# Fused attention and two MLPs: behind attention all five engines take their instructions in written order, with weight words moved and a third word tile

## The chip, the cores and the metric

The kernel runs on one core of a Trainium2 chip. The metric is the device time of one execution in microseconds (us), as a median over runs. The core has five engines with a queue each: TensorE (PE, matmuls), VectorE (DVE), ScalarE (ACT), GpSimd (POOL) and SyncE (SP, which here issues almost all DMAs).

## The reference

Block-causal attention over 4 batches x 8 heads x 576 positions x 64, whose output is a matrix of 2304 tokens x 512; then two MLPs one after the other, each 512 -> 2048 -> 512. The weights are float64 on the host.

```
x = attention(q, k, v)                                  # 2304 x 512
h = x @ w_in;  g = max(h, 0) + alpha * min(h, 0);  y = g @ w_out      # first MLP
h = y @ w_in2; g = where(h > 0, h, exp(min(h, 0)) - 1); out = g @ w_out2   # second MLP
```

## The kernel before

**Tokens and chunks.** The tokens are cut into five units u of 512, 512, 512, 512 and 256 tokens, the 2048 hidden features into 16 chunks f of 128. The program has two parts. In the first, attention runs together with chunks 0 to 3 of the first MLP for units 0, 1 and 2 (generator `l1_beside`). The change concerns the second part, "behind attention": a list of 148 steps, one for each (kind, unit, chunk). In order: A3 (steps 0 to 7), A4 (8 to 15), B2 (16 to 27), B0 (28 to 39), B1 (40 to 51), D4 (52 to 59), D3 (60 to 67), then the second MLP, C2 (68 to 83), C0, C1, C3, C4. A letter with a digit is a kind and its unit; unit 4 has 256 columns.

**A step.** At step i PE makes h(i), 12 matmuls into one of three "h" banks of PSUM (L551 for the first MLP, L605 for the second). ACT and DVE make the gate of it: in the first MLP `neg` (ACT, L528), `g` (DVE, L531), its rounded copy (ACT, L535) and the remainder (POOL, L89); in the second `e` by exp (ACT, L609), two DVE operations (L610, L611), a copy (ACT, L614) and the remainder (DVE, L89). The two results go into one tile of a ring: "gs" has four, "gsl" three, and steps use them by turns. Then PE takes h(i)'s tile of three steps ago (`lag = 3`) and makes y(i-3), up to four groups of matmuls that add into "acc" banks (L655, L630). PE thus always runs h(i), y(i-3), h(i+1), y(i-2) and so on.

**Joins.** A kind's and unit's last y closes its sums, three steps after its last h. I call that step a join: step 10 (A3 to A4), 18 (A4 to B2), 30, 42, 54, 62 and 70 (D3 to C2). There the four sums leave the acc banks: `to_z` copies them at steps 10 and 18 (ACT for m = 0 and 2, tile `z`; DVE for m = 1 and 3, tile `zl`; L93 and L95), and stores them by DMA (L558); later joins add an earlier `z` (DVE, L662), round and store (L663, L665). There are five acc banks in a ring, of which a unit takes four, so that the next unit's second sum needs a bank that the join must have emptied.

**Weight words.** `load_w(layer, f, r)` brings one "word": 512 KB of float64, which arrives in a `wraw` tile (three of them, L123) and is turned into a rounded weight and its remainder: ACT twice (L133, L134), DVE three times (L138, L139, L143), POOL once (L148), ACT (L158), DVE (L89, out `w`). `later(n, ...)` puts each of these stages into a coming tick; a step has two ticks, so the stages stand one half step apart in the source, and the first stands `arrival[0]` ticks after the load. Word number k thus needs `wraw` from the load to L148 and a `wword` tile from L133 to the last L89. `w_at` says at which step which word is loaded.

**Order.** In the first part `manual_schedule` names all five engines: each takes instructions as the source emits them. In the second part only PE is named; for ACT, DVE, POOL and SP a planner, with its own estimates of times, has put instructions into an order at build time. On the chip an engine's queue is what was built.

Of the kernel before, what the change touches and what calls it, by code (L numbers as in the profile page):

```python
# [9 lines left out]
F32 = mybir.dt.float32  # L10
# [4 lines left out]
ALU = mybir.AluOpType  # L15
# [4 lines left out]
P = 128  # L20
B, H, S, D = 4, 8, 576, 64
NT, DM, DFF = 2304, 512, 2048
# [14 lines left out]
def f32(ap):  # L37
    return ap.bitcast(F32)
# [3 lines left out]
def attention_moe_kernel(ctx: ExitStack, tc: tile.TileContext, qT, kT, v_a, v_b, w1, w2, alpha, out):  # L42
    nc = tc.nc
    pe, act, dve, pool_e = nc.tensor, nc.scalar, nc.vector, nc.gpsimd
# [4 lines left out]
    wraw_p = ctx.enter_context(pool("wraw", 2))  # L49
# [18 lines left out]
    def ring(name, *banks):  # L68
        rings[name] = list(banks)
# [18 lines left out]
    def low_part(eng, out, x, high):  # L88
        return {"v": dve, "p": pool_e}[eng].tensor_tensor(out=out, in0=x, in1=f32(high), op=ALU.subtract)  # L89

    def copy(eng, out, x, scale=None):
        if eng == "a":
            return act.copy(out, x) if scale is None else act.mul(out, x, scale)  # L93
        if eng == "v":
            return dve.tensor_copy(out, x) if scale is None else dve.tensor_scalar(out, x, scale, None, ALU.mult)  # L95
        return pool_e.tensor_scalar(out, x, 1.0 if scale is None else scale, 1.0, ALU.mult, ALU.mult)  # L96
# [6 lines left out]
    def later(ticks, emit):  # L103
        due.setdefault(tick[0] + ticks, []).append(emit)
# [13 lines left out]
    def load_w(layer, f, r):  # L118
        if r == 0:
            wt[layer, f] = w_pools[min(f // 4, 2)].tile([P, 2, 2 * DM], F32R, tag="w", name="w")  # L120
        t = wt[layer, f]
        raw = wraw_p.tile([P, 2 * DM], U32, tag="wraw", name="wraw", bufs=3)
        nc.sync.dma_start(out=raw, in_=(w1, w2)[layer][f, :, r * DM:(r + 1) * DM].bitcast(U32))  # L123
        pairs = raw.rearrange("p (n t) -> p n t", t=2)
        low, high = pairs[:, :, 0], pairs[:, :, 1]
        units = low.bitcast(I32)
        hi, lo = (t[:, k, r * DM:(r + 1) * DM] for k in range(2))
        word = []

        def first():  # L130
            w = wraw_p.tile([P, DM], F32, tag="wword", name="wword")
            word.append(w)
            act.activation(out=w, in_=high.bitcast(F32), func=AF.Abs)  # L133
            act.activation(out=units, in_=low, func=AF.Copy, scale=2.0 ** -29)  # L134

        def bits():
            w, wi = word[0], word[0].bitcast(U32)
            dve.tensor_scalar(w, w, F64_MIN, F64_MAX, ALU.max, ALU.min)  # L138
            dve.tensor_scalar(wi, wi, 3, 0x3FFFFFF8, ALU.logical_shift_left, ALU.bitwise_and)  # L139

        def sign():
            wi = word[0].bitcast(U32)
            dve.scalar_tensor_tensor(  # L143
                out=wi, in0=high, scalar=0xC0000000, in1=wi, op0=ALU.bitwise_and, op1=ALU.bitwise_or)

        def rounded():
            w = word[0].bitcast(I32)
            pool_e.tensor_tensor(out=w, in0=w, in1=units, op=ALU.add)  # L148

        def last():  # L150
            low_part("v", lo, word[0], hi)
            ready.add((layer, f, r))
        lead = arrival[0]
        later(lead, first)
        later(lead + 1, bits)
        later(lead + 1, sign)
        later(lead + 2, rounded)
        later(lead + 3, lambda: act.copy(hi, word[0]))  # L158
        later(lead + 4, last)

    arrival = [2]
# [21 lines left out]
    ap2 = att.enter_context(pool("att2", 2))  # L183
# [18 lines left out]
        return d // 2, slice(4 * (d % 2), 4 * (d % 2) + 4)  # L202

    def raw_tiles():
        return [ap2.tile([P, S], F32, tag=f"{x}raw", name=f"{x}raw", bufs=4) for x in "qk"]

    def load_early(d):
        b, hs = duo(d)
# [15 lines left out]
    def load_late(n):  # L224
        b, p = PAIRS[n]
        st[n]["raw"] = q, k = raw_tiles()
        hs = slice(2 * p, 2 * p + 2)
        nc.sync.dma_start(out=k, in_=kT[b, hs].rearrange("e p s -> (e p) s"))
        nc.sync.dma_start(out=q[:, 256:], in_=qT[b, hs].rearrange("e p s -> (e p) s")[:, 256:])

    def load_late_v(n):
        b, p = PAIRS[n]
# [5 lines left out]
    def high_parts(n):  # L238
        s = st[n]
        q, k = s["raw"]  # L240
        for which, x, scale in (("q", q[:, 256:], 0.125), ("k", k, None)):
            s[which] = [ap2.tile([P, x.shape[1]], F32R, tag=f"{which}{t}", name=f"{which}{t}") for t in "hl"]
            copy("p", s[which][0], x, scale)
        low_part("p", s["k"][1], k, s["k"][0])

    def low_parts(n):
        s = st[n]
        hi, lo = s["q"]
        dve.scalar_tensor_tensor(out=lo, in0=s["raw"][0][:, 256:], scalar=0.125, in1=f32(hi), op0=ALU.mult, op1=ALU.subtract)

    def diagonal(n):
        for low in range(2):
# [189 lines left out]
    for n in range(NP):  # L442
        k = AT[n, EARLY]
# [3 lines left out]
        for i in (2, 3, 4):  # L447
            k = AT[n, i]
# [12 lines left out]
    for n in range(NP):  # L461
        k = NP + 3 * n
# [83 lines left out]
    def l1_h(u, f):  # L546
        n, x = UNITS[u], x1[u]
        h = bank[take("h")][:, :n]
        for kc in range(KC):
            for t, (wp_, xp_) in enumerate(PASSES):  # L550
                pe.matmul(h, w_in(0, f, wp_, kc), x[:, xp_, kc, :n],  # L551
                          start=kc == 0 and t == 0, stop=kc == KC - 1 and t == 2)
        return h
# [46 lines left out]
    def l2_h(u, f):  # L600
        n, x = UNITS[u], x1[u]
        h = bank[take("h")][:, :n]
        for kc in range(KC):
            for t, (wp_, xp_) in enumerate(PASSES):
                pe.matmul(h, w_in(1, f, wp_, kc), x[:, xp_, kc, :],  # L605
                          start=kc == 0 and t == 0, stop=kc == KC - 1 and t == 2)
        e = gp.tile([P, 512], F32, tag="g", name="e", bufs=3)[:, :n]
        gs = gs_tile()[:, :, :n]
        act.activation(out=e, in_=h, func=AF.Exp)  # L609
        dve.tensor_scalar(e, e, 1.0, -1.0, ALU.min, ALU.add)  # L610
        dve.scalar_tensor_tensor(out=e, in0=h, scalar=0.0, in1=e, op0=ALU.max, op1=ALU.add)  # L611

        def parts():
            act.copy(gs[:, 0, :], e)  # L614
            low_part("v", gs[:, 1, :], e, gs[:, 0, :])
        later(1, parts)
        return gs
# [50 lines left out]
    ET = mybir.EngineType  # L668
    with tc.manual_schedule(engines={ET.PE, ET.Activation, ET.DVE, ET.Pool, ET.SP}):
# [29 lines left out]
        k = LEAD  # L699
        for u, (a, b, c, d) in enumerate(stretches):  # L700
            assert a >= X_DONE[u]
            parts = l1_beside(u)
            for first, end, n in ((a, b, 2 * FA), (c, d, 2 * KC)):
                slots(k, first)
                k = first
                for j in range(n):
# [3 lines left out]
                    k = to  # L710
# [1 line left out]
        assert not held and not halves  # L712


    with tc.manual_schedule(engines={ET.PE}):


        att.close()
        ps = ctx.enter_context(pool("ps_all", 1, space=PSUM))
        bank[:] = [ps.tile([P, 512], F32, name=f"bank{i}") for i in range(8)]  # L720
        w_pools.append(ctx.enter_context(pool("w2", NF - 8)))
        late_pools.append(ctx.enter_context(pool("late", 1)))
        ring("h", 5, 6, 7)
        ring("acc", *range(5))
        units = [("A", 3), ("A", 4)] + [("B", u) for u in (2, 0, 1)] + [
            ("D", u) for u in (4, 3)] + [("C", u) for u in (2, 0, 1, 3, 4)]
        fs = CHUNKS
        steps = [(k, u, f) for k, u in units for f in fs[k]]
        first_of = {}
        for i, (k, u, f) in enumerate(steps):  # L730
            first_of.setdefault((k, u), i)
        lag = 3
        words = sorted((3 * r + f, f, r) for f in range(8) for r in range(2))
        w_at = dict(zip((1, 3, 4, 6, 7, 8, 10, 12, 14, 16, 18, 19, 21, 22, 24, 25), ((0, 8 + f, r) for _, f, r in words)))
        freed = first_of["B", 1] + 8
        for i in range(16):
            f, r = divmod(i, 2)
            w_at[first_of["B", 0] + 2 * i if i < 8 else freed + 2 * i - 16] = 1, f, r
            w_at[first_of["C", 2] - 4 + i] = 1, 8 + f, r
        gs = {}  # L740
        for i in range(len(steps) + lag):
            if i in w_at:
                arrival[0] = 4 if i < first_of["C", 2] - 4 else 2
                load_w(*w_at[i])
            if i < len(steps):
                k, u, f = steps[i]
                if f == fs[k][1]:
                    n = units.index((k, u)) + 1
                    if n < len(units) and units[n] != ("D", u):
                        (load_x2 if units[n][0] == "C" else load_x1)(units[n][1])  # L750
                gs[i] = l2_h(u, f) if k == "C" else l1_gate(f, l1_h(u, f), UNITS[u])
            end_tick()
            if i >= lag:
                k, u, f = steps[i - lag]
                if k == "C":
                    l2_y(u, f, gs.pop(i - lag))
                else:
                    l1_y(k, u, f, gs.pop(i - lag))
            end_tick()
# [32 lines left out]
```

## Time and profile before

| | |
|---|---|
| median of 3 runs | 1006.86 us (1006.8 to 1007.06) |
| the profiled execution's own time | 1007.81 us |
| its span, first to last instruction | 1006.0 us |
| PE busy | 961.3 us (96% of the span), granted clock 0.989 |
| DVE, ACT, POOL busy | 541.1, 441.9, 343.9 us |
| stretch 258 to 612 us (A, B, D): PE, DVE, ACT, POOL busy | 343.67, 196.31, 159.59, 156.82 of 354.00 us |
| stretch 612 to 1001 us (C): the same | 386.52, 155.90, 102.75, 12.00 of 389.00 us |

Read it as follows. PE is busy nearly always, and a matmul's end is modelled, so what counts is the distance from one start to the next and the idle times that a row gives in brackets. The time of an engine other than PE counts only where PE stands still for it.

### The profile page before, as it was taken

What the parts mean: (1) busy time and instruction counts of PE and PEld (TensorE: products, weight loads), DVE (VectorE), ACT (ScalarE), POOL (GpSimd) and SP (SyncE); (2) the same over time, 40 slices, a digit from 0 to 9 for tenths busy, and PEclk for the clock granted to TensorE, in tenths of its full rate; (3) what the DMA queues carried; (4) which work ended last, traced back from release to release, by engine and by line L of the source; (5) the groups of instructions that cost most, each with busy time, mean ns of one, the idle gap of its engine ahead of it and who ended that gap; (6) DMA issues with size and microseconds to landing.
All of it is one profiled execution on the core that took longest, in us unless ns stands there. A gap on an engine that the chain in (4) does not pass through costs nothing.

```text
span 1006.0 us, 13778 instructions
## 1 busy us (share of the span) xinstructions
PE 961.3 (96%) x5008; PEld 774.1 (77%) x5008; DVE 541.1 (54%) x1012; ACT 441.9 (44%) x985; POOL 343.9 (34%) x401
## 2 busy tenths in 40 slices
PE   5789999999997999999999999999999999999997
PEld 3456777666787788888889887888888888888896
DVE  5878676776498871311862489634333333333343
ACT  6876576776465653222553365422222222222222
POOL 4788576694255553322553363200000000000000
PEclk9999999999998999999999999999999999999999
DMA  6553533625546552401535555002002100200010
GB/s 216 178 183 140 154 102 114 224 72 157 183 140 237 199 183 84 141 0 42 186 119 177 163 201 174 29 1 111 15 1 84 42 1 1 84 1 0 1 43 21
DMA packets 55525, 105.76 MB, mean 105 GB/s; under 512 B 11041, under 2 KB 29473, under 8 KB 54305
## 3 DMA queue, kind: packets, MB, share of 16 engines
q1 hardware_dynamic: 55168, 104.62, 31.4%
q8 instruction: 39, 0.64, 0.3%
q10 hardware_dynamic: 288, 0.26, 0.1%
q14 instruction: 30, 0.24, 0.1%
HBM read 76.55 MB, written 28.31 MB: 104 GB/s over the span
## 4 chain that ended last, share of the span: by engine, by line
PE 73%; DVE 11%; ACT 6%; DMA 4%; POOL 3%; issue 2%; SPq 0%; POOLq 0%; ACTq 0%; DVEq 0%
PE bank L630 20%; PE bank L605 19%; PE bank L655 11%; PE bank L551 11%; PE bank L423 3%; PE bank L582 3%; DMA wraw<-w 2%; DVE w L89 2%; PE bank L570 2%; DVE wword L143 2%; PE pair L276 2%; DVE wword L139 2%; PE bank L363 2%; DVE wword L138 1%; ACT wword L133 1%
## 5 line engine op out<-in xcount | busy, mean ns | idle before, releaser
L605 PE MATMUL bank<-x,w 128*128 128x512 f32 (+1 forms) x960 | 210.4, 368 | 0.0
L605 PEld LDWEIGHTS bank<-x,w 128*128 128x128 f32 x960 | 169.7, 189 | 31.4
L551 PE MATMUL bank<-x,w 128*128 128x512 f32 (+1 forms) x816 | 177.2, 367 | 1.3 <-DVE xtail L89 1.3
L551 PEld LDWEIGHTS bank<-x,w 128*128 128x128 f32 x816 | 143.0, 191 | 26.2 <-ACT xtail L429 1.4
L610 DVE TENSOR_SCALAR e<-e 128x512 f32<-128x512 f32 (+1 forms) x80 | 33.1, 413 | 172.1 <-ACT e L609 172.1
L609 ACT ACTIVATE e<-bank 128x512 f32<-128x512 f32 (+1 forms) x80 | 44.4, 555 | 184.8 <-PE bank L605 184.8
L148 POOL TENSOR_TENSOR wword<-wword,wraw 128x512 int32<-128x512 int32 x64 | 93.7, 1465 | 77.3 <-issue 23.5
L531 DVE SCALAR_TENSOR_TENSOR g<-neg,beta,bank 128x512 f32<-128x512 f32 (+1 forms) x80 | 55.1, 689 | 117.8 <-ACT neg L528 117.7
L630 PE MATMUL bank<-w,gsl 128*128 128x512 f32 x432 | 106.4, 393 | 2.2 <-DVE z L662 2.2
L630 PE MATMUL bank<-w,gs 128*128 128x512 f32 x432 | 104.6, 389 | 0.0
L655 PE MATMUL bank<-gsl,w 128*128 128x512 f32 (+1 forms) x408 | 91.0, 371 | 9.1 <-ACT z L93 6.5
L96 POOL TENSOR_SCALAR p<-p,stat 128x128 f32<-128x128 f32 (+4 forms) x144 | 81.3, 580 | 48.5 <-DVE stat L334 32.7
L630 PEld LDWEIGHTS bank<-w,gsl 128*128 128x128 f32 x432 | 81.2, 190 | 19.5 <-DVE z L662 2.6
L630 PEld LDWEIGHTS bank<-w,gs 128*128 128x128 f32 x432 | 80.6, 188 | 16.4
L89 POOL TENSOR_TENSOR gs<-g,gs 128x512 fp32r<-128x512 f32 (+1 forms) x46 | 59.0, 1283 | 90.0 <-ACT gs L535 89.9
L655 PEld LDWEIGHTS bank<-gsl,w 128*128 128x128 f32 x408 | 71.7, 192 | 23.0 <-ACT z L93 7.1
L325 ACT ACTIVATE p<-pair,stat 128x128 f32<-128x128 f32 (+4 forms) x144 | 78.3, 557 | 24.0 <-DVE stat L298 21.7
L655 PE MATMUL bank<-gs,w 128*128 128x512 f32 (+1 forms) x408 | 87.8, 364 | 0.0
L655 PEld LDWEIGHTS bank<-gs,w 128*128 128x128 f32 x408 | 70.6, 189 | 12.2
L528 ACT ACTIVATE neg<-bank 128x512 f32<-128x512 f32 (+1 forms) x80 | 44.1, 552 | 79.5 <-PE bank L551 78.3
L89 DVE TENSOR_TENSOR w<-wword,w 128x512 fp32r<-128x512 f32 x64 | 57.1, 896 | 16.5 <-ACT w L158 15.9
L298 DVE TENSOR_REDUCE stat<-pair 128x2 f32<-128x256 f32 (+3 forms) x80 | 63.1, 806 | 4.2 <-PE pair L281 2.2
(80 smaller groups left out, 1256.7 us busy)
## 6 DMA issues: line engine op xcount, KB each, us to landing
wraw<-w SPq DMA_DIRECT2D x64, 512.0 KB, 4.0
xd<-x SPq DMA_DIRECT2D x4, 2048.0 KB, 8.5
x<-xd SPq DMA_DIRECT2D x16, 512.0 KB, 7.6
x<-yd SPq DMA_DIRECT2D x4, 2048.0 KB, 7.9
vraw<-v_a SPq DMA_DIRECT2D x24, 256.0 KB, 3.3
kraw<-kT SPq DMA_DIRECT2D x16, 288.0 KB, 3.8
yd<-gs SPq DMA_DIRECT2D x8, 512.0 KB, 3.7
yd<-gsl SPq DMA_DIRECT2D x8, 512.0 KB, 5.4
```

Of the source, the lines that this page charges most:

```text
L89: return {"v": dve, "p": pool_e}[eng].tensor_tensor(out=out, in0=x, in1=f32(high), op=ALU.subtract)
L96: return pool_e.tensor_scalar(out, x, 1.0 if scale is None else scale, 1.0, ALU.mult, ALU.mult)
L148: pool_e.tensor_tensor(out=w, in0=w, in1=units, op=ALU.add)
L298: peak = lambda out, x, axis=AX.X: dve.tensor_reduce(out=out, in_=x, axis=axis, op=ALU.max, negate=True)
L325: act.activation(out=out, in_=x, func=AF.Exp, bias=stat[:, k:k + 1], accum_out=stat[:, SUMS + 2 * k:SUMS + 2 * k + 1])
L528: act.activation(out=neg, in_=h, func=AF.Relu, scale=-1.0)
L531: dve.scalar_tensor_tensor(out=g, in0=neg, scalar=beta[:, f:f + 1], in1=h, op0=ALU.mult, op1=ALU.add)
L551: pe.matmul(h, w_in(0, f, wp_, kc), x[:, xp_, kc, :n], start=kc == 0 and t == 0, stop=kc == KC - 1 and t == 2)
L605: pe.matmul(h, w_in(1, f, wp_, kc), x[:, xp_, kc, :], start=kc == 0 and t == 0, stop=kc == KC - 1 and t == 2)
L609: act.activation(out=e, in_=h, func=AF.Exp)
L630: pe.matmul(acc, gs[:, gp_, tg * P:(tg + 1) * P], w_out(1, f, wp_, 0, DM), start=f == 0 and t == 0, stop=f == NF - 1 and t == 2)
L655: pe.matmul(acc, w_out(0, f, wp_, m * P, P), gs[:, gp_, :n], start=first and t == 0, stop=last and t == 2)
```

## The change

The second part's `manual_schedule` now names all five engines. `w_at` has new steps, in the diff. The first six words of the part are loaded in steps 0 to 5 with 6 ticks from load to first stage (before: 4). `wword` gets a third tile. To make room the late pairs' `q` is kept in a tile of 512 columns and not 576, at columns 0 to 319. No instruction of computation is added or removed; PE's order is the same row for row.

```diff
-            w = wraw_p.tile([P, DM], F32, tag="wword", name="wword")
+            w = wraw_p.tile([P, DM], F32, tag="wword", name="wword", bufs=3)
...
-        return [ap2.tile([P, S], F32, tag=f"{x}raw", name=f"{x}raw", bufs=4) for x in "qk"]
+        return [ap2.tile([P, n], F32, tag=f"{x}raw", name=f"{x}raw", bufs=4) for x, n in (("q", 512), ("k", S))]
...
-        nc.sync.dma_start(out=q[:, 256:], in_=qT[b, hs].rearrange("e p s -> (e p) s")[:, 256:])
+        nc.sync.dma_start(out=q[:, :320], in_=qT[b, hs].rearrange("e p s -> (e p) s")[:, 256:])
...
-    with tc.manual_schedule(engines={ET.PE}):
+    with tc.manual_schedule(engines={ET.PE, ET.Activation, ET.DVE, ET.Pool, ET.SP}):
...
-        w_at = dict(zip((1, 3, 4, 6, 7, 8, 10, 12, 14, 16, 18, 19, 21, 22, 24, 25), ((0, 8 + f, r) for _, f, r in words)))
-        freed = first_of["B", 1] + 8
-        for i in range(16):
-            f, r = divmod(i, 2)
-            w_at[first_of["B", 0] + 2 * i if i < 8 else freed + 2 * i - 16] = 1, f, r
-            w_at[first_of["C", 2] - 4 + i] = 1, 8 + f, r
+        w_at = dict(zip((0, 1, 2, 3, 4, 5, 9, 11, 13, 17, 18, 20, 21, 22, 24, 25), ((0, 8 + f, r) for _, f, r in words)))
+        w_at.update(zip((29, 31, 33, 35, 37, 41, 43, 45, 47, 48, 49, 53, 55, 57, 61, 62),
+                        ((1, f, r) for f in range(8) for r in range(2))))
+        w_at.update(zip((*range(64, 69), *range(71, 82)), ((1, 8 + f, r) for _, f, r in words)))
...
-                arrival[0] = 4 if i < first_of["C", 2] - 4 else 2
+                arrival[0] = 6 if i < 6 else 4 if i < first_of["C", 2] - 4 else 2
```

ACT's queue at the join of step 10 (A3 to A4), before; `neg<-bank_2977` is h(10)'s gate, `bank_2971` and `bank_2973` hold A3's sums 0 and 2:

```order
L158 CAST w<-wword 128x512
L133 ACTIVATE wword<-wraw 128x512
L134 ACTIVATE wraw<-wraw 128x512
L535 CAST gs<-g 128x256
L133 ACTIVATE wword<-wraw 128x512
L134 ACTIVATE wraw<-wraw 128x512 x2
L528 ACTIVATE neg<-bank_2977 128x256
L93 COPY z<-bank_2971 128x512
L158 CAST w<-wword 128x512
L535 CAST gsl<-g 128x256
L93 COPY z<-bank_2973 128x512
```

The same place in the changed kernel:

```order
L158 CAST w<-wword 128x512
L535 CAST gs<-g 128x256
L528 ACTIVATE neg<-bank_2977 128x256
L535 CAST gsl<-g 128x256
L93 COPY z<-bank_2971 128x512
L93 COPY z<-bank_2973 128x512
L133 ACTIVATE wword<-wraw 128x512
L134 ACTIVATE wraw<-wraw 128x512
```

The two copies now stand together, ahead of any stage of a word; five instructions on words (L133 twice, L134 three times) that stood ahead of the first copy behind the last L158 are gone from there.

DVE's queue at the join of step 70 (D3 to C2), before; `bank_2975`, `bank_2971`, `bank_2972`, `bank_2973` hold D3's four sums, `bank_2977` is h(70):

```order
L89 TENSOR_TENSOR gs<-e,gs 128x512
L138 TENSOR_SCALAR wword<-wword 128x512
L662 TENSOR_TENSOR z<-bank_2975,z 128x512
L610 TENSOR_SCALAR e<-e 128x512
L662 TENSOR_TENSOR zl<-bank_2971,zl 128x512
L139 TENSOR_SCALAR wword<-wword 128x512
L662 TENSOR_TENSOR z<-bank_2972,z 128x512
L611 SCALAR_TENSOR_TENSOR e<-bank_2977,e 128x512
L89 TENSOR_TENSOR w<-wword,w 128x512
L662 TENSOR_TENSOR zl<-bank_2973,zl 128x512
L89 TENSOR_TENSOR gs<-z,gs 128x512
```

The same place in the changed kernel:

```order
L610 TENSOR_SCALAR e<-e 128x512
L611 SCALAR_TENSOR_TENSOR e<-bank_2977,e 128x512
L89 TENSOR_TENSOR gsl<-e,gsl 128x512
L662 TENSOR_TENSOR z<-bank_2975,z 128x512
L89 TENSOR_TENSOR gs<-z,gs 128x512
L662 TENSOR_TENSOR zl<-bank_2971,zl 128x512
L662 TENSOR_TENSOR z<-bank_2972,z 128x512
L89 TENSOR_TENSOR gs<-z,gs 128x512
L662 TENSOR_TENSOR zl<-bank_2973,zl 128x512
L89 TENSOR_TENSOR w<-wword,w 128x512
```

The whole gate of h(70), remainder included, and the remainders of the sums now stand ahead of later sums; the words' stages L138 and L139 no longer stand between.

## Rows read from the trace of the kernel before

**Rows 1.** Waits of PE, 258 us to the end: total, times, longest.

```profile
PE bank L655 <- ACT z L93: 6.5, 2, 4.9
PE bank L630 <- DVE z L662: 2.2, 1, 2.2
```

**Rows 2.** PE timeline, undisturbed: start, us, line, operation, count.

```profile
324.08 1.60 PE L655 MATMUL bank<-gsl,w 128*128 128x256 f32 x12
325.52 1.60 PE L551 MATMUL bank<-x,w 128*128 128x256 f32 x12
...
402.96 2.88 PE L551 MATMUL bank<-x,w 128*128 128x512 f32 x12
405.68 2.88 PE L655 MATMUL bank<-gsl,w 128*128 128x512 f32 x12
```

**Rows 3.** PE timeline, the join A3 to A4.

```profile
310.22 0.52 PE L655 MATMUL bank<-gsl,w 128*128 128x256 f32 x3
...
321.21 1.60 PE L655 MATMUL bank<-gs,w 128*128 128x256 f32 x12
```

**Rows 4.** PE timeline, the join A4 to B2.

```profile
346.57 0.84 PE L655 MATMUL bank<-gsl,w 128*128 128x512 f32 x3
...
356.72 2.88 PE L655 MATMUL bank<-gs,w 128*128 128x512 f32 x12
```

**Rows 5.** PE timeline, the join D3 to C2.

```profile
613.82 0.84 PE L630 MATMUL bank<-w,gsl 128*128 128x512 f32 x3
...
623.60 2.88 PE L630 MATMUL bank<-w,gs 128*128 128x512 f32 x12
```

**Rows 6.** PE timeline, the end of attention and steps 0 to 4.

```profile
247.36 0.52 PE L363 MATMUL bank<-ident,p 128*128 128x128 f32 x3 [0.79 <-ACT pt L93]
...
259.61 11.16 PE L551 MATMUL bank<-x,w 128*128 128x512 f32 x48 [1.26 <-DVE xtail L89]
270.61 0.40 PE L655 MATMUL bank<-gsl,w 128*128 128x512 f32 x1
...
274.49 2.88 PE L551 MATMUL bank<-x,w 128*128 128x512 f32 x12
```

**Rows 7.** ACT groups on words, 255 to 360 us: count | busy, mean ns | idle before, releasers.

```profile
L133 ACT ACTIVATE wword<-wraw 128x512 f32<-128x512 f32 x22 | 14.8, 670 | 9.5 <-DVE w L89 7.7 <-DMA wraw<-w 1.8
L134 ACT ACTIVATE wraw<-wraw 128x512 int32<-128x512 uint32 x21 | 14.3, 679 | 14.5 <-DMA wraw<-w 13.7 <-DVE pt L95 0.8
...
L158 ACT CAST w<-wword 128x512 fp32r<-128x512 f32 x21 | 12.9, 619 | 9.9 <-POOL wword L148 9.9
```

**Rows 8.** ACT timeline at the join A3 to A4.

```profile
310.51 0.62 ACT L158 CAST w<-wword 128x512 fp32r<-128x512 f32 x1 [2.83 <-POOL wword L148]
...
315.02 0.59 ACT L93 COPY z<-bank 128x512 f32<-128x512 f32 x1
```

**Rows 9.** DVE timeline at the join D3 to C2.

```profile
612.08 0.43 DVE L138 TENSOR_SCALAR wword<-wword 128x512 f32<-128x512 f32 x1 [0.40 <-ACT wword L133]
...
614.70 1.51 DVE L138 TENSOR_SCALAR wword<-wword 128x512 f32<-128x512 f32 x1
616.13 0.68 DVE L662 TENSOR_TENSOR z<-bank,z 128x512 f32<-128x512 f32 x1
```

**Rows 10.** POOL timeline at the same join.

```profile
614.41 1.52 POOL L148 TENSOR_TENSOR wword<-wword,wraw 128x512 int32<-128x512 int32 x1 [3.73 <-ACT wword L133]
```

**Rows 11.** ACT timeline around the end of attention.

```profile
240.54 0.69 ACT L134 ACTIVATE wraw<-wraw 128x512 int32<-128x512 uint32 x1 [1.93 <-DMA wraw<-w]
...
264.78 0.66 ACT L134 ACTIVATE wraw<-wraw 128x512 int32<-128x512 uint32 x1 [5.90 <-DMA wraw<-w]
```

**Rows 12.** Page, DMA issues: count, KB each, median us to landing.

```profile
wraw<-w SPq DMA_DIRECT2D x64, 512.0 KB, 4.0
```

**Rows 13.** Page, costliest groups: gate and remainder of the first MLP.

```profile
L531 DVE SCALAR_TENSOR_TENSOR g<-neg,beta,bank 128x512 f32<-128x512 f32 (+1 forms) x80 | 55.1, 689 | 117.8 <-ACT neg L528 117.7
...
L89 POOL TENSOR_TENSOR gs<-g,gs 128x512 fp32r<-128x512 f32 (+1 forms) x46 | 59.0, 1283 | 90.0 <-ACT gs L535 89.9
```

More of the change, by code (lines that the diff above doesn't have):

```diff
@@ L240, in high_parts @@
         q, k = s["raw"]
-        for which, x, scale in (("q", q[:, 256:], 0.125), ("k", k, None)):
+        for which, x, scale in (("q", q[:, :320], 0.125), ("k", k, None)):
             s[which] = [ap2.tile([P, x.shape[1]], F32R, tag=f"{which}{t}", name=f"{which}{t}") for t in "hl"]
@@ L248, in low_parts @@
         hi, lo = s["q"]
-        dve.scalar_tensor_tensor(out=lo, in0=s["raw"][0][:, 256:], scalar=0.125, in1=f32(hi), op0=ALU.mult, op1=ALU.subtract)
+        dve.scalar_tensor_tensor(out=lo, in0=s["raw"][0][:, :320], scalar=0.125, in1=f32(hi), op0=ALU.mult, op1=ALU.subtract)
     def diagonal(n):
```

## The prediction

> **What bounds the kernel now.** I read the waits of PE behind attention first. They are few: 6.5 us for ACT's copies of `z`, 2.2 us for DVE's adds [rows 1]. PE's order is the same before and after, so the time behind attention is PE's undisturbed pace plus what it loses at these places. The pace comes from starts in quiet stretches: twelve matmuls of 512 columns take 405.68 - 402.96 = 2.72 us, twelve of 256 columns 325.52 - 324.08 = 1.44 us [rows 2]. Next I read the PE timeline at each place where it waits, and took the way from the disturbed start to the next undisturbed one, less that pace; this counts the idle time and also the matmuls that run longer after it:
>
> - Join of A3 and A4: from y(8) at 310.22 to y(9) at 321.21 are 10.99 us [rows 3]; y(8) and h(12), 256 columns each, should take 2.88. Lost 8.11.
> - Join of A4 and B2: 346.57 to 356.72 are 10.15 us [rows 4]; y(16) and h(20) should take 5.44. Lost 4.71.
> - Join of D3 and C2: 613.82 to 623.60 are 9.78 us [rows 5], against 5.44. Lost 4.34.
> - First y of the part: 270.61 to 274.49 are 3.88 us [rows 6], against 2.72. Lost 1.16.
> - End of attention: 0.79 us for a copy on ACT [rows 6].
>
> Together 19.11 us. There is one more, the 1.26 us before step 0's first matmul, which waits for attention's last output [rows 6].
>
> Then I looked at why. An engine's instructions stand in one queue, and what waits at its head holds the rest. From 255 to 360 us ACT stood idle ahead of words' stages for 9.5 + 14.5 + 9.9 = 33.9 us, for DVE, for loads and for POOL [rows 7]. At the first join ACT sat 2.83 us for a word at POOL, until 310.51, and copied A3's first sum only at 315.02 [rows 8]. That sum was complete before 310.22, as PE was already at A4's first y then [rows 3]. So `z` is late because the planner put words ahead of it. At D3 to C2 it is DVE: L138 stands ahead of the first add and takes 1.51 us, since POOL's L148 runs from 614.41 to 615.93 meanwhile; alone the same instruction takes 0.43 [rows 9, 10]. Near 264.78 ACT waited 5.90 us for a load with the gate of h(0) behind it, and at 240.54 it waited 1.93 us so with attention's work behind it [rows 11].
>
> **The change, part by part.** *Joins of steps 10 and 18.* Let T be the end of h(10). In the new order ACT has the gate's `neg`, the copy and then both `z`, with no word between. An ACT operation of a full tile takes about 0.6 (L158: 619 ns [rows 7]), a `g` 0.69 [rows 13]. The first `z` is done by T + 0.6 + 0.7 + 0.6 + 0.6 = T + 2.5, even with full widths. PE wants its bank for the second sum of y(8): y(7) 2.72, h(11) 1.44, one sum of four 0.36, so T + 4.5. The other copies on ACT and DVE end near T + 3.2, for T + 4.9 and later. At step 18 the want is 1.44 + 2.72 + 0.68 = T + 4.8. Both losses go: -8.11 and -4.71. What hides the copies is one h; without it 2 us would show.
>
> *Join of step 70.* With T the end of h(70), DVE does `e` by T + 1.7 (ACT 0.6, DVE 0.4 and 0.7), waits for ACT's copy (2.3), makes the remainder (2.9), add 0 (3.6), waits for that copy (4.2) and makes its remainder (4.9), add 1 (5.6), add 2 (6.3). PE wants the banks at 5.44 + 0.68 = T + 6.1, then 6.8 and 7.5. It fits by 2.5, 1.2 and 1.2 us. But each collision with POOL adds 1.51 - 0.43 = 1.1 us [rows 9], and words come at one per step until step 68, so DVE may arrive late. From below 0 remains, from above all 4.34. I take 0.7, since one collision fits and a second does not quite: -3.6.
>
> [...]
>
> *Joins of steps 30, 42, 54, 62.* No wait of PE stands there now, and the same walk (no `e`; the remainder of g is POOL's) ends add 2 at T + 4.7 for a want of 7.5, at step 54 (256 columns behind it) of 2.72 + 1.44 + 1.08 = 5.2. There a collision would cost 0.6; I take 0.
>
> *A wait that the change adds.* A join takes two tiles of the gsl ring for its sums. The fourth sum's copy goes into the tile that y(i-2) reads, and PE runs that one step later. In written order ACT stands at it for some 5 us, with the next word and neg(i+1) behind; two steps on, the copy of g(i+2) waits in the same way for y(i), until T + 3 x 5.44 + 2.72 = T + 19.0. Who waits for these? y(i+2) wants its tile at T + 5 x 5.44 = T + 27.2, and the copy and POOL's 1.3 [rows 13] are over at T + 21. h(i+6) wants the bank of h(i+3) at T + 29.9, and its gate, with a word's 1.35 us on ACT ahead, is through by T + 23. PE does not see it: 0, with 6 us to spare.
>
> *SP.* Stores of `z` at a join now hold the loads behind them. The word of step 11 is issued near T + 3.5 and lands 4.0 us later [rows 12], or about T + 8 behind the stores; its L133 stands behind the gate of h(12), at T + 8.4 to 9. Words loaded in steps 0 to 5 have three steps, 16 us, from load to first stage. Each word is through about two steps before its first matmul. 0; a late one costs 5 us only where it eats these two steps.
>
> *Start.* Steps 0 to 2 now have no word's stage on ACT before them, so neg(0) follows h(0) at once: -1.16. Attention's last copies lose the two hoisted L134: -0.79. The third `wword` tile takes away L133's wait for DVE, 7.7 us of ACT there [rows 7], which lies beside PE; the narrower `q` moves the same bytes. Both 0 in themselves.
>
> Sum: -8.11 - 4.71 - 3.6 - 1.16 - 0.79 = -18.4. The profiled execution took 1007.81 us, its span 1006.0. It would take 989.4. The runs' median lies 0.95 us below that execution, so **988.4 us**.
>
> **The rivals.** *One join keeps its wait.* DVE comes to step 70 a few us behind, since with a word per step it has about 4 us of work plus collisions in 5.44. For it: the stretch's L138 of 1.51. Against it: no bits are placed in step 70. 988.4 + 3.6 = 992.0.
>
> *Loads hold ACT.* L133 and L134 waited 15.5 us for loads in that stretch [rows 7]; in written order a late one holds the gates behind it, and in A4's short steps the slack is three steps of 2.88, about 8.6 us. One wait such as the 5.90 [rows 11] fits, two in a row do not: some 6 us back, 994 to 995.
>
> *Slower: the gsl ring.* If a later gate, not only the copy, were held until the third step after a join, PE would stand at each of the five joins behind step 18. The slack of 6 us decides: a wait longer than 5 + 6 = 11 us reaches PE. A hold of a whole three-step round, 16 us, would cost 5 us each at five joins, 25 us: about 1013. Against it: the copy is freed by y(i), which itself waits for nothing behind it.
>
> [...]
>
> *It does nothing.* The waits could come from loads or banks whatever the order: 1007. Against it: the sum that PE waited for was complete some 5 us before its copy.
>
> **How the numbers follow.** All joins clear, 0.70, with a range of its own of 986.5 to 990.5 (step 70's 0 to 2 us, and about 1 us either way for attention's end). One join kept 0.13. Loads 0.09. Gsl ring 0.05. Nothing 0.03. A measurement of this kernel tells about 0.2%, 2 us, from no change. Faster 0.92, same 0.03, slower 0.05. The range, 986 to 994.5, takes in the first two cases and half of the third.
>
> **What would show it.** Right: after the profile, PE's waits behind attention hold only the 1.26 us, at most 2 us at step 70, and the starts between steps 8 and 20 are 1.44 and 2.72 us apart; ACT's `z` at step 10 ends within 3 us of h(10). ACT's idle time ahead of the join's fourth copy and of the copy two steps later, some 5 us each, shows the ring, with no PE wait after it. Wrong: PE waits for `neg` or `g` at h, or for `w`, or for a POOL remainder at a y, or new waits in attention's last 15 us.

## The result and the profile after

The changed kernel takes **989.41 us** (median of 6 runs, 988.59 to 990.09); the kernel before, beside it, 1006.44 us (6 runs, 1004.85 to 1007.06). The ratio is 0.9834, 95% interval 0.9821 to 0.9846. The profiled execution took 989.64 us, its span is 987.8 us (before 1006.0), PE is busy for 955.5 us of it (97%) at a granted clock of 0.995 (before 0.989), and the median landing time of a word is 4.6 us (before 4.0 [rows 12]).

Waits of PE from 255 us to the end, which answer to [rows 1] (total, times, longest):

```profile
PE bank L551 <- DVE xtail L89: 1.3, 1, 1.3
PE bank L551 <- DVE g L531: 0.6, 1, 0.6
```

The copies of `z` and the adds, 6.5 and 2.2 us before, are gone from the list. The first row is the one at step 0, which was there before; the second is new. The PE timeline (start, us, line, operation, count, idle time) at step 0, at the joins of steps 10, 18 and 70, and at the new wait, step 60 (h of D3's first chunk):

```profile
258.78 11.16 PE L551 MATMUL bank<-x,w 128*128 128x512 f32 x48 [1.27 <-DVE xtail L89]
269.78 2.88 PE L655 MATMUL bank<-gsl,w 128*128 128x512 f32 x12
272.50 2.88 PE L551 MATMUL bank<-x,w 128*128 128x512 f32 x12
...
308.24 1.60 PE L655 MATMUL bank<-gsl,w 128*128 128x256 f32 x12
...
311.12 1.60 PE L655 MATMUL bank<-gs,w 128*128 128x256 f32 x12
...
336.48 2.88 PE L655 MATMUL bank<-gsl,w 128*128 128x512 f32 x12
...
341.92 2.88 PE L655 MATMUL bank<-gs,w 128*128 128x512 f32 x12
...
538.77 1.60 PE L655 MATMUL bank<-gsl,w 128*128 128x256 f32 x12
541.01 3.01 PE L551 MATMUL bank<-x,w 128*128 128x512 f32 x12 [0.64 <-DVE g L531]
543.86 1.60 PE L655 MATMUL bank<-gs,w 128*128 128x256 f32 x12
...
599.94 2.88 PE L630 MATMUL bank<-w,gsl 128*128 128x512 f32 x12
...
605.38 2.88 PE L630 MATMUL bank<-w,gs 128*128 128x512 f32 x12
```

From y(8) to y(9) are 311.12 - 308.24 = 2.88 us, where [rows 3] show 10.99; at step 18, 5.44 where [rows 4] show 10.15; at step 70, 605.38 - 599.94 = 5.44 where [rows 5] show 9.78; behind the first y, 2.72 where [rows 6] show 3.88. All four run at the undisturbed pace. Step 0 starts 259.61 - 258.78 = 0.83 us earlier. Step 60 loses 2.24 - 1.44 = 0.80, and 0.10 more in the matmuls behind it. So 0.83 + 8.11 + 4.71 + 1.16 + 4.34 - 0.90 = 18.25 us, against 1006.0 - 987.8 = 18.2 us of span.

ACT at the join of step 10; h(10) ends at 304.21:

```profile
304.31 0.39 ACT L528 ACTIVATE neg<-bank 128x256 f32<-128x256 f32 x1 [2.05 <-PE bank L551]
305.25 0.41 ACT L535 CAST gsl<-g 128x256 fp32r<-128x256 f32 x1 [0.55 <-DVE g L531]
305.56 0.58 ACT L93 COPY z<-bank 128x512 f32<-128x512 f32 x1
306.32 0.59 ACT L93 COPY z<-bank 128x512 f32<-128x512 f32 x1 [0.18 <-PE bank L655]
306.81 0.68 ACT L133 ACTIVATE wword<-wraw 128x512 f32<-128x512 f32 x1
```

The two `z` are done 1.9 and 2.7 us after h(10)'s end, within the 3 us forecast, and no word stands ahead. Before, the same first copy ran at 315.02 [rows 8]. DVE at the join of step 70, with h(70) ending at 594.66:

```profile
597.84 0.68 DVE L662 TENSOR_TENSOR z<-bank,z 128x512 f32<-128x512 f32 x1
...
599.82 0.68 DVE L662 TENSOR_TENSOR zl<-bank,zl 128x512 f32<-128x512 f32 x1
600.42 0.68 DVE L662 TENSOR_TENSOR z<-bank,z 128x512 f32<-128x512 f32 x1
601.79 1.28 DVE L89 TENSOR_TENSOR gs<-z,gs 128x512 fp32r<-128x512 f32 x1 [0.69 <-ACT gs L663]
```

Adds 0, 1 and 2 (L662) end 3.9, 5.8 and 6.4 us after h(70), for a want of 6.1, 6.8 and 7.5. One remainder takes 1.28 (0.69 for the one at 599.21), but behind the adds that count.

The new wait starts on SP. The word loaded in step 55 stands there behind the stores of join 54; ACT then waits for it with the gate of h(57) behind, and h(60) writes into the bank that this gate reads (SP rows: start, us in the queue, line; then ACT):

```profile
532.19 0.51 SPq L665 DMA_DIRECT2D yd<-gsl  x1
532.75 0.60 SPq L123 DMA_DIRECT2D wraw<-w  x1
...
538.92 0.68 ACT L133 ACTIVATE wword<-wraw 128x512 f32<-128x512 f32 x1 [1.85 <-DMA wraw<-w]
...
540.08 0.36 ACT L528 ACTIVATE neg<-bank 128x256 f32<-128x256 f32 x1
```

### The profile page after: what moved, and what is told of

Read it like the earlier page. It is cut to its first block, busy times and chain, and to the rows that moved or that the text cites. A ratio compares the mean times of both kernels' runs of the same rounds, so it can differ in the third digit from the quotient of the medians.

```text
span 987.8 us, 13766 instructions
## 1 busy us (share of the span) xinstructions
PE 955.5 (97%) x5008; PEld 770.9 (78%) x5008; DVE 545.7 (55%) x1012; ACT 437.4 (44%) x985; POOL 337.9 (34%) x401
## 4 chain that ended last, share of the span: by engine, by line
PE 85%; DVE 4%; POOL 3%; ACT 3%; issue 2%; DMA 1%; SPq 1%; POOLq 0%; ACTq 0%; DVEq 0%
PE bank L605 20%; PE bank L630 20%; PE bank L551 16%; PE bank L655 16%; PE bank L423 3%; PE bank L582 3%; PE pair L276 2%; PE bank L363 2%; PE bank L570 2%; ACT p L325 1%; POOL p L96 1%; DVE stat L298 1%; PE pair L281 1%; POOL gs L89 1%; PE bank L369 1%
## 5 line engine op out<-in xcount | busy, mean ns | idle before, releaser
L148 POOL TENSOR_TENSOR wword<-wword,wraw 128x512 int32<-128x512 int32 x64 | 93.3, 1458 | 79.1 <-DVE wword L143 61.6
L655 PE MATMUL bank<-gsl,w 128*128 128x512 f32 (+1 forms) x408 | 87.8, 364 | 0.0
L89 POOL TENSOR_TENSOR gs<-g,gs 128x512 fp32r<-128x512 f32 (+1 forms) x46 | 56.8, 1235 | 87.3 <-ACT gs L535 87.3
L89 DVE TENSOR_TENSOR w<-wword,w 128x512 fp32r<-128x512 f32 x64 | 67.1, 1048 | 16.6 <-ACT w L158 16.6
L143 DVE SCALAR_TENSOR_TENSOR wword<-wraw,wword 128x512 uint32<-128x512 uint32 x64 | 72.4, 1131 | 2.2
```

Of the source, the lines that this page charges most:

```text
L143: dve.scalar_tensor_tensor(out=wi, in0=high, scalar=0xC0000000, in1=wi, op0=ALU.bitwise_and, op1=ALU.bitwise_or)
L655: pe.matmul(acc, w_out(0, f, wp_, m * P, P), gs[:, gp_, :n], start=first and t == 0, stop=last and t == 2)
```

## The experiments

Three edits can be taken apart: who orders the queues, the third `wword` tile, and the steps of the words (with `arrival[0]`). The narrower `q` is in every cell of the table but the two with two tiles and old steps. No run has it alone; the program built with it alone has the same instructions in the same order on all five engines as before. This is what the eight combinations took, as ratios to the kernel before run beside each:

| word tiles | word steps | planner's order | written order |
|---|---|---|---|
| 2 | old | 1 (before) | 1.0111 (1.0086 to 1.0135) |
| 2 | new | 0.9987 (0.9976 to 0.9998) | 0.9976 (0.9964 to 0.9988) |
| 3 | old | 1.0125 (1.0094 to 1.0156) | 0.9905 (0.9886 to 0.9925) |
| 3 | new | 1.0093 (1.0061 to 1.0124) | 0.9834 (0.9821 to 0.9846), the change |

### The changed kernel with the planner's order

```diff
-    with tc.manual_schedule(engines={ET.PE, ET.Activation, ET.DVE, ET.Pool, ET.SP}):
+    with tc.manual_schedule(engines={ET.PE}):
```

> The changed kernel with the new word steps, the third word tile and the narrower q, but with ACT, DVE, POOL and SP behind attention ordered by the planner again (only PE in written order). Theory A (the written order carries the gain, since the planner puts stages of words ahead of the joins' copies): 998 to 1007 us, with PE waits for ACT's z at steps 10 and 18 back, some 4 to 8 us each. Theory B (the new word steps carry it, whatever orders the engines): 988 to 991 us and no such wait.

1015.41 us, ratio 1.0093. PE waits 8.9 us for ACT's `z` (5.4 at step 10), 2.3 for DVE's `z` and 1.7 for `zl`. That is the first theory's kind, with the waits at steps 10 and 18 back, but above its range: with the tile and the word steps and without the order the kernel is slower than before, which I had not expected.

### The order and the third tile, with the old word steps

```diff
-        w_at.update(zip((29, 31, 33, 35, 37, 41, 43, 45, 47, 48, 49, 53, 55, 57, 61, 62),
-                        ((1, f, r) for f in range(8) for r in range(2))))
...
+            w_at[first_of["B", 0] + 2 * i if i < 8 else freed + 2 * i - 16] = 1, f, r
```

The other word steps and `arrival[0]` are as before too.

> The changed kernel with all five engines in written order, but the words at the steps of before, and 4 ticks from load to first stage in steps 0 to 5. Theory A (order): most of the gain stays, 989 to 996 us; at step 10 one L158 more stands ahead of z, which the 2 us of margin cover; at step 70 a word's L138, L139, L143 (1.5 us, and 1.1 more for a collision with POOL) stand ahead of the adds and eat its 1.2 us of margin, 0.5 to 2 us of wait. Theory B (word steps): 1003 to 1008 us, with the waits of before at steps 10, 18 and 70.

996.82 us, ratio 0.9905: most of the gain stays, a little less than the first theory had. Steps 10 and 18 are clear, and so is step 70, where I had expected the loss. What is lost is at step 62:

```profile
557.17 0.84 PE L655 MATMUL bank<-gsl,w 128*128 128x512 f32 x3
561.96 3.87 PE L655 MATMUL bank<-gsl,w 128*128 128x512 f32 x9 [3.95 <-DVE z L662]
...
568.41 1.75 PE L655 MATMUL bank<-gs,w 128*128 128x512 f32 x7
```

11.24 us where 5.44 would do: 5.80. On DVE a word's three stages stand ahead of the first add, from 558.90 to 561.57, the last of them L143 with 1.76 us. At the join of step 54 another 1.18 is lost, for an add of `zl`. So the written order keeps exactly what the source says, and the new word steps, which have no load in steps 52, 54, 58 and 60, keep words off these two joins.

### The changed kernel with two word tiles

```diff
-            w = wraw_p.tile([P, DM], F32, tag="wword", name="wword", bufs=3)
+            w = wraw_p.tile([P, DM], F32, tag="wword", name="wword", bufs=2)
```

> The changed kernel with two word tiles again in place of three. Theory A (the third tile is worth nothing in itself, since L133's wait for the last stage of the word two before it lies beside PE): 989 to 991 us, ACT waits for DVE's last word stage again, no wait of PE for it. Theory C (in written order the third tile keeps ACT from standing in front of the gates): 993 to 1000 us, PE waits for gates in the stretches with a word per step.

1003.04 us, ratio 0.9976, above the range of the theory that it bears out (C): a tile that I had priced at nothing is worth 1003.04 - 989.41 = 13.6 us. The place is C2, where a word is loaded in nearly each step up to step 81. PE, then ACT, then DVE and POOL there:

```profile
649.94 3.01 PE L605 MATMUL bank<-x,w 128*128 128x512 f32 x12 [1.07 <-DVE e L611]
...
656.74 3.01 PE L605 MATMUL bank<-x,w 128*128 128x512 f32 x12 [1.07 <-DVE e L611]
...
674.15 3.88 PE L605 MATMUL bank<-x,w 128*128 128x512 f32 x10 [3.01 <-DVE w L89]
...
647.01 0.67 ACT L133 ACTIVATE wword<-wraw 128x512 f32<-128x512 f32 x1 [3.26 <-DVE w L89]
...
648.12 0.58 ACT L609 ACTIVATE e<-bank 128x512 f32<-128x512 f32 x1
...
653.81 0.66 ACT L133 ACTIVATE wword<-wraw 128x512 f32<-128x512 f32 x1 [3.27 <-DVE w L89]
...
645.13 1.80 DVE L89 TENSOR_TENSOR w<-wword,w 128x512 fp32r<-128x512 f32 x1
648.74 0.43 DVE L610 TENSOR_SCALAR e<-e 128x512 f32<-128x512 f32 x1 [1.81 <-ACT e L609]
...
651.64 1.54 POOL L148 TENSOR_TENSOR wword<-wword,wraw 128x512 int32<-128x512 int32 x1 [5.27 <-DVE wword L143]
651.93 1.80 DVE L89 TENSOR_TENSOR w<-wword,w 128x512 fp32r<-128x512 f32 x1
```

Read it as a ring. L133 of a word waits for the tile that the last stage of the word two before it gives free (DVE, L89, ended 646.93). The gate's `e` stands behind L133 on ACT, DVE's part of the gate waits for `e`, and DVE's next L89 of a word stands behind that. One round takes 653.81 - 647.01 = 6.80 us, while an h and a y take PE only 5.44. Of the 1.36 us between them 1.12 come from one collision: at 651.93 L89 starts 0.29 us behind POOL's L148 and takes 1.80 us, against 0.68 where no L148 runs (in the changed kernel at 603.59). Without it a round would take about 5.68 us, an estimate from these rows, which is still longer than a step. With three tiles L133 waits for a word one round further back, and the ring is open: in the changed kernel ACT's waits from 600 to 700 us hold none of L133 for L89; here there are nine of them with 29.3 us. From 640.25 to 677.87 PE makes five steps in 37.62 us for 27.20, so 10.42 are lost there. The last step, h(83), has 6.04 of them: words too come only every 6.80 us, and PE waits 3.01 for the last one's `w` (the row at 674.15). Another 3.12 are lost at step 70, where PE waits for DVE's adds.

### The third tile alone

The diff has only the parts on `wword` and on `q`.

> The kernel before with only the third word tile and the narrower q that makes room for it; the planner orders ACT, DVE, POOL and SP, the words stand at their old steps. Theory C (the third tile is worth its 13 us only in written order, where ACT stands at L133 with a gate behind it): 1003 to 1007 us, the waits at steps 10, 18 and 70 still there. Theory D (the third tile is the change's gain whatever the order): 990 to 997 us.

1018.98 us, ratio 1.0125. The waits are there, as theory C had it, but the kernel is slower than before, which neither theory had. With a third tile the planner lets words run further ahead. PE waits 6.6 us for DVE's `z` at step 70, and for ACT's `z` (total, times, longest):

```profile
PE bank L655 <- ACT z L93: 9.3, 2, 5.0
```

And the timeline of DVE, then ACT, up to step 10's copies:

```profile
309.50 1.79 DVE L89 TENSOR_TENSOR w<-wword,w 128x512 fp32r<-128x512 f32 x1
...
311.81 0.47 DVE L531 SCALAR_TENSOR_TENSOR g<-neg,beta,bank 128x256 f32<-128x256 f32 x1
...
307.95 0.37 ACT L528 ACTIVATE neg<-bank 128x256 f32<-128x256 f32 x1
312.31 0.41 ACT L535 CAST gsl<-g 128x256 fp32r<-128x256 f32 x1 [3.99 <-DVE g L531]
...
319.48 1.07 ACT L93 COPY z<-bank 128x512 f32<-128x512 f32 x2
```

DVE has word stages ahead of a `g` whose `neg` was ready at 308.3, and ACT waits for that `g`. Behind it ACT still has L133 and L134 of three words and three L158 ahead of the copies, which start 7.17 us later. So the same tile costs 11 to 13 us under the planner and gives 14 to 21 in written order (differences in the table's columns).

### The order alone

Of the diff, only the `manual_schedule` line is kept.

> The kernel before with only the written order for all five engines: two word tiles, the words at their old steps. Theory C (order, third tile and word steps need each other): the waits for z at steps 10 and 18 are gone, but in steps 64 to 80, a word each, PE waits for e about 1.4 us per step, and the word stages of those steps hold the join of step 70: 1000 to 1009 us. Theory A as first stated (the third tile and the word steps add little to the order): 989 to 997 us.

1016.74 us, ratio 1.0111, slower than before and above the range of theory C, which had the mechanism. Steps 10 and 18 are clear even so. The loss stands later: PE waits 4.7 us for DVE's `z` at step 70 and 3.9 at step 62, 5.2 us for `e` in C2 (5 times) and 3.0 for `w`, and C2's h run 6.80 us apart, the ring of the changed kernel with two tiles.

### The new word steps alone

> The missing cell of the table: the planner orders ACT, DVE, POOL and SP behind attention, as before; two word tiles, as before; the new word steps. Theory A (each of the three edits pays only with the other two; words in more or earlier steps give the planner more word stages to set ahead of the joins' copies): slower than before, 1009 to 1018 us, with PE's waits at the joins of steps 10 and 18 for ACT's copy of z, 5 us each or more, and no waits of PE in C2, since the planner spaces the word stages there. Theory B (the word steps are good by themselves): 1000 to 1006 us, with the join of step 70 clear, which the new steps leave free of a load.

(The changed kernel with the planner's order and two tiles.) 1003.37 us, ratio 0.9987. The second theory had the time right and the first the place: step 10 still waits 4.7 us for `z`, step 18 only 0.8, and step 70 1.0. The interval (0.9976 to 0.9998) just excludes no change: by themselves the word steps gain next to nothing, but do no harm, which was not in my first theory.

### PE and ACT alone in written order

```diff
-    with tc.manual_schedule(engines={ET.PE, ET.Activation, ET.DVE, ET.Pool, ET.SP}):
+    with tc.manual_schedule(engines={ET.PE, ET.Activation}):
```

> The changed kernel with only PE and ACT in written order behind attention; DVE, POOL and SP are ordered by the planner, with three word tiles and the new word steps as in the changed kernel. Theory A (the queue that mattered is ACT's, with words ahead of the copies of z; DVE's gate work suffers only because the planner lets ACT run ahead on words): the joins of steps 10 and 18 are clear, step 70 loses at most 2 us, 988 to 993 us. Theory B (all queues must agree, since with three tiles the planner sets word stages ahead of the gate on DVE whatever ACT does): PE waits for DVE's g or for z at the later joins, 996 to 1012 us.

988.72 us, ratio 0.9819 (0.9803 to 0.9836). Waits of PE from 230 us to the end, the second still in attention:

```profile
PE bank L551 <- DVE xtail L89: 1.3, 1, 1.3
PE bank L363 <- ACT pt L93: 0.3, 1, 0.3
```

No join and no gate is left in the list. The first theory holds: with ACT's queue written, the third tile and the new word steps, the planner's order of DVE, POOL and SP does no harm. That order is another one than the written: from 255 to 360 us ACT's L158 waited 8.5 us for POOL in the changed kernel, and here not at all. PE sees neither.

### Two gsl tiles

```diff
-            return late_pools[0].tile([P, 2, 512], F32R, tag="gsl", name="gsl", bufs=3)
+            return late_pools[0].tile([P, 2, 512], F32R, tag="gsl", name="gsl", bufs=2)
```

> The changed kernel with two tiles in the gsl ring in place of three. A join's fourth copy on ACT then goes into the tile of h(i)'s own gate, which PE reads at step i+3, T + 19.0 us behind the end of h(i), with the gate of h(i+1) behind it; h(i+4) wants that gate at T + 19.0. Theory A (only the slack keeps such holds from PE): the slack is gone, 3 to 5 us at each of the joins 30, 42, 54, 62 and 70, 1003 to 1014 us in all, PE waiting for g or for POOL's remainder one step past each. Rival (ACT's stands at a join do not matter): 989 to 991 us.

997.1 us, ratio 0.9905 (0.9883 to 0.9927): 7.7 us more. ACT's waits from 258 to 600 us, at the copies of the join:

```profile
ACT gsl L663 <- PE bank L655: 18.0, 4, 5.5
ACT gsl L663 <- DMA yd<-gsl: 15.2, 4, 4.0
```

The mechanism of the ring rival is there: held copies reach PE, as 3.3 us for DVE's `g` and 0.6 for POOL's remainder behind the join of step 54, and as about 1 us each for `z`, `zl` and `e` from step 70 on. I had expected a loss at each of five joins; those of steps 30, 42 and 62 stay clear, so the cost is below the range that I gave it. With three tiles ACT's waits there are 4.6 us for PE in two places and 10.5 for DVE's `zl` in six, 2.3 at the longest, and PE sees none.

### SP by the planner; the load of step 53 two steps earlier; both

```diff
-    with tc.manual_schedule(engines={ET.PE, ET.Activation, ET.DVE, ET.Pool, ET.SP}):
+    with tc.manual_schedule(engines={ET.PE, ET.Activation, ET.DVE, ET.Pool}):
```

```diff
-        w_at.update(zip((29, 31, 33, 35, 37, 41, 43, 45, 47, 48, 49, 53, 55, 57, 61, 62),
+        w_at.update(zip((29, 31, 33, 35, 37, 41, 43, 45, 47, 48, 49, 51, 55, 57, 61, 62),
```

> The changed kernel, but SP's queue behind attention ordered by the planner; PE, ACT, DVE and POOL in written order. Theory A (the gain lies in the order of ACT and DVE; SP's is worth under 1 us): 988 to 991 us. Rival (SP's written order, with loads behind the joins' stores, carries a part of it): 993 us or more, or with loads earlier 987 us and no ACT wait for loads at the joins of steps 54 and 70.

> The changed kernel with one word's load moved from step 53, just ahead of the join of step 54, to step 51. If the one wait that the change added (0.6 us before h(60), for a gate that stands on ACT behind a late load) comes from that load's place behind the join's stores, it goes: 0.9 us less than the changed kernel, 988 to 989 us, and no PE wait behind step 0 at all. Rival (the load is late because all loads around the join are slow): the wait stays, 989 to 990 us.

> The changed kernel with SP left to the planner and the load of step 53 moved to step 51, the two variants that gave 988.3 and 988.9 us together. If both only remove the same 0.6 us wait of PE at h(60): 988.0 to 989.0 us, below the changed kernel by 0.4 to 1.4 us. If they add up: 987.0 to 988.0 us.

988.27 us, ratio 0.9827 (0.9802 to 0.9851); 988.92 us, 0.9834 (0.9810 to 0.9858); both together 988.8 us, 0.984 (0.9827 to 0.9854). The wait of 0.64 us at step 60 is gone in all three, and the times can't be told from the changed kernel's. These rows tell the first two apart: the load of step 55's word and its L133 with SP planned, and then this L133 with the load of step 53 moved:

```profile
511.51 0.33 SPq L123 DMA_DIRECT2D wraw<-w  x1
...
537.29 0.68 ACT L133 ACTIVATE wword<-wraw 128x512 f32<-128x512 f32 x1
```

```profile
537.81 0.68 ACT L133 ACTIVATE wword<-wraw 128x512 f32<-128x512 f32 x1 [5.04 <-DMA wraw<-w]
```

With SP planned the load goes out at 511.51, ahead of the stores, and not at 532.75 behind them, and L133 waits for nothing: this shows the cause. The moved load is the wrong one. Step 55's still stood behind the stores and ACT still waited for it; it landed 5.5 us after its issue and not 6.2, so that h(60) starts 0.27 us late in place of 0.80. What made it quicker stays open. Both together are not better than either: step 70 loses 0.62 us there, with a wait of 0.29 for DVE's `zl`.

### The first gate into another ring

```diff
         ring("acc", *range(5))
+        turn[0] += 1
```

The added line stands at the start of the second part, so that step 0 writes a `gs` tile.

> The changed kernel with one thing more: the turn of the two rings is moved on by one, so that step 0's gate goes into a tile of gs, which stands in memory of its own, and not of gsl, which lies where attention's tiles lay. Theory A (ACT's 4.5 us of waiting ahead of the part's first gsl copy comes from the store of attention's last output tile, from whose memory gsl is made): ACT's first copy of g comes some 4 us earlier, near 263 us, and the wait for that store moves to step 1's copy or is gone; the time stays at 989 plus or minus 1.5 us, since PE wants y(0) only at 269.8 us. Theory B (the copy waits for the gate itself): the copy stays near 267 us.

989.37 us, ratio 0.9842 (0.9829 to 0.9856). ACT in the changed kernel (two rows), then in this one (two):

```profile
261.87 0.60 ACT L528 ACTIVATE neg<-bank 128x512 f32<-128x512 f32 x1 [3.82 <-PE bank L551]
267.02 0.62 ACT L535 CAST gsl<-g 128x512 fp32r<-128x512 f32 x1 [4.55 <-DMA xd<-xtail]
```

```profile
263.56 0.62 ACT L535 CAST gs<-g 128x512 fp32r<-128x512 f32 x1 [0.81 <-DVE g L531]
...
267.30 0.62 ACT L535 CAST gsl<-g 128x512 fp32r<-128x512 f32 x1 [1.82 <-DMA xd<-xtail]
```

The first copy comes 3.5 us earlier and the first `gsl` copy, now step 1's, still waits for the store of attention's last output. So the memory of the `gsl` ring is what holds it, not the gate; PE's time doesn't change.

## Why the prediction was right, and the step that was wrong

The time (988.4 forecast, 989.41 measured; for the profiled execution 989.4 and 989.64) and the sum of 18.4 us (18.25) hold. The two large terms, the joins of steps 10 and 18, hold for the reason given. That the whole sum fits so closely is in part luck, as smaller terms missed both ways. Step by step:

- **Joins of steps 10 and 18, -8.11 and -4.71: right.** Both losses are gone whole, and in no run with ACT's queue written does PE wait for ACT's `z`, whatever the tiles and the word steps.
- **Join of step 70, -3.6: right in kind, 0.7 too small.** All of the 4.34 went. I had kept 0.7 for a second collision ahead of the adds; there was none, and the join's one lengthened operation (1.28 us) fell behind add 2. But the clear join isn't the work of the order alone, which leaves a wait of 4.7 us there; it takes the third tile too (clear with the old word steps, 3.12 us lost with two tiles).
- **Third word tile, "0 in itself": wrong, the step that failed.** I took its wait only where the trace of before had it, from 255 to 360 us, and there two tiles do suffice in written order. I never walked a step of C2 under the new order with a word each. Priced with the other two edits there, the tile is worth 13.6 us; order and word steps without it give 0.9976. My sum came out since I took all edits together, the tile among them; that it was there was luck as far as my reasons go. The pieces don't add: by the table's ratios order alone costs 11 us and the tile alone nearly 13.
- **Start, -1.16: right in size, wrong in cause.** neg(0) does follow h(0) at once (261.87, before 265.34), but that isn't what freed y(0). The copy behind it waits 4.55 us, until 267.02, for the store of attention's last output to land. My walk had not seen this store, and it held the same copy before, until 269.84, whatever neg(0) did:

```profile
269.84 0.62 ACT L535 CAST gsl<-g 128x512 fp32r<-128x512 f32 x1 [0.52 <-DMA xd<-xtail]
```

The store was issued at 260.56 before and at 258.96 after, and landed 9.3 and 8.0 us later. Before, a word's load stood ahead of it on SP, at 259.65; what made its landing quicker stays open. y(0) at 269.78 was met with little to spare, since the copy ended at 267.64 and POOL's remainder ran from 267.77 for 1.29. So the size was luck.

- **End of attention, -0.79: too large by 0.33.** Of the wait 0.33 us stayed, with ACT's copy now waiting 0.55 for PE's own L369 and not for a word, so 0.46 were gained. That step 0 starts 0.83 earlier has another 0.37 in it, which were there already in attention's first 50 us (a matmul at 47.01 before is at 46.63 after). The change claims nothing there, and the runs that keep the written order start step 0 anywhere from 258.13 to 259.09.
- **SP, 0: off by 0.9 us.** A store at a join does hold a load, as I wrote (the load issued at 532.75 behind the stores goes out at 511.51 with SP planned), but the slack that I gave it ("a late one costs 5 us only where it eats these two steps") was the word's own. What suffers first is the gate queued behind L133, in a stretch of 256 columns, where a step takes 2.88. PE's wait for `g` at an h is one of the signs of being wrong that I had listed; it came, but small.
- **Gsl ring, 0: right.** The waits on ACT are 2.3 us at most where I had 5. Two tiles, at 7.7 us, show that the danger was real.
- **The rivals.** One join that keeps its wait, with DVE late at step 70, comes with two word tiles (3.12 us), beside a loss in C2 that no rival had; loads that hold ACT reach PE once, with 0.9 us and not 6; the gsl ring needs one tile less; no effect is excluded by the interval.

In both orders the traces show ACT holding an operation behind others of its queue: in the planned one a `z` whose sum was complete before 310.22 [rows 3] stands behind words until 315.02 [rows 8], in the written one with two tiles an `e` stands until 648.12 behind L133's wait of 3.26 us for a tile.

## What to carry to other kernels

When an engine's order is fixed by hand, walk one round of the densest stretch through all queues and rings of buffers: an operation that waits for a buffer holds what is queued behind it (here L133's 3.26 us of waiting held the gate's `e`), and where the chain from the wait back to the giving free of that buffer is longer than a step, it sets the pace (6.80 us for 5.44 here) until one more buffer opens it. Order, buffers and places of loads have to be priced together; here the order alone and the tile alone each made the kernel over 1% slower. Write by hand the queue whose waits reach the bound engine; here that was ACT's, and with the tile and the word steps in place, leaving three others to the planner cost nothing that can be measured.

## What was not expected of the hardware

- Beside POOL's L148 (1.54 us at 651.64) DVE's L89 on a word, started 0.29 us behind it, takes 1.80 us in place of 0.68. With two tiles the pair meets round after round in C2 (L89 at 645.13, 651.93 and 658.73, 1.80 us each). That fits the collision of 1.1 us that the prediction worked out of [rows 9, 10], but it comes in step with the ring, not by chance.
- A join cost PE more than the list of its waits says. At step 10 the waits before were 4.92 us for `z` and 0.78 for `zl`, in a loss of 8.11. Nearly all of the rest is matmuls that ran longer behind the waits; the twelve of h(12) take 321.21 - 318.90 = 2.31 us where 1.44 are undisturbed:

```profile
317.45 1.65 PE L655 MATMUL bank<-gsl,w 128*128 128x256 f32 x6 [0.78 <-DVE zl L95]
318.90 2.48 PE L551 MATMUL bank<-x,w 128*128 128x256 f32 x12
```

PE had stood still for 4.92 us, and from 315.60 to 321.20 its mean granted clock is 0.53; from 321.20 to 340 it is 1.00. In the changed kernel it is 1.00 all the way from 290 to 320 us, with PE busy throughout.
